# Block-sparse attention with a Fourier mixing layer: k turned by DMA instead of by TensorE

## The chip, the cores and the metric

The kernel runs on one core of one Trainium2 chip. The metric is the device time of one execution in microseconds (us). In this document PE is TensorE (matrix products), PEld its weight loads, DVE is VectorE, ACT is ScalarE, POOL is GpSimd, and SP is SyncE, which here only issues DMA transfers.

## The reference

Two parts follow each other. The first is attention for 4 batches, 8 heads, 768 positions and a head size of 64, in which every query sees its own block of 64 keys and the three blocks whose mean key has the highest product with it:

```
k_rep = k.reshape(B, H, 12, 64, D).mean(axis=3)
gate_scores = einsum('bhsd,bhnd->bhsn', q, k_rep), minus 1e9 where the block lies ahead
selected = top 3 blocks by gate_scores, and the own block
scores = (q @ k.T) / sqrt(D) where selected and causal, else -1e9
x = softmax(scores) @ v, heads side by side: [4, 768, 512]
```

The second works on x batch by batch: the real part of a 2-D Fourier transform over positions and channels is added to x (u = x + real(fft2(x))), u is normalised over its 512 channels, and out = u + relu(un @ w_ch1) @ w_ch2, with w_ch1 of [512, 2048] and w_ch2 of [2048, 512].

## The kernel before

The work of attention is cut into 16 pairs of heads, kk = 0 to 15, four pairs to a batch. A pair goes through these stages, each a function of the kernel:

- load_qk and load_v fetch q, k and v of the pair in f32 with the positions on the 128 partitions (six tiles of 128 positions), over the SP queue. The buffers of q, k and v hold two pairs.
- stage_A(kk, who, g) transposes three tiles at a time on PE with an f32 identity (line 279): who = 0 is q, who = 1 is k. For k, DVE sums each block of 64 columns into kr12 (line 292) and three or four copies by ACT, the fourth by DVE for the pairs before EARLY = 7, cast the transposed k to f16 into kI (lines 309 and 311). kI is the weight operand of the scores: rows 0 to 63 are k, rows 64 to 75 hold for each block n the value -60000 in the columns of block n (IndN, loaded once into each of three slots).
- stage_B makes the gate scores: q's transpose times the block sums. For the pairs before SPLIT = 8 both are f32 (line 323, five matmuls). From pair 8 on q and the sums, scaled by 64, are each split into two f16 parts (lines 287, 288, 304 and 305), and the products are ten f16 matmuls (line 331) and one more addition on DVE. DVE then takes the largest eight of each query and head (line 340) and turns the comparison with the third into a 0/1 mask gmp.
- stage_C transposes the mask on PE (line 354, gt) into the rows 64 to 75 of qg, the moving operand of the scores, so that an unselected block gets -60000 added.
- stage_S computes one of three score sections of a head (line 386) into one of two PSUM buffers (sc), and ACT takes the exponential (line 391). For the pairs before EARLY the causal triangle is added by PE (line 390), later DVE multiplies it in (line 397).
- stage_AV multiplies by v (line 412) with a column of ones for the sum, DVE divides, and fold prepares the Fourier transform's symmetric halves on POOL or DVE.

When a batch has its four pairs, the mixing part follows as a chain of units: stage_S1 (line 480 and 484) and stage_S2 (507, 508, 515) are the transforms, stage_N the norm, stage_T the transposes of the normed rows (562), then bulk units stage_M1 (ha and hb, line 578) and stage_M2 (ch, line 592) for the two products with w_ch1 and w_ch2.

The order of the instructions on PE and POOL is written out by the kernel (a manual schedule). The main loop goes through the pairs; each pair has six slots p = 0 to 5 with one score section, and a table says in which slot the stages of the neighbouring pairs stand:

```
USUAL = dict(A1=0, AV1=1, A0=2, C=3, AV0=4, B=5)
NORM = dict(A1=4, AV1=1, A0=5, C=3, AV0=4, B=6)
```

A1 is stage A for k of pair kk + 2, A0 the same for q with the loads of pair kk + 4 behind it, B the gates of pair kk + 2, C the masks of pair kk + 1. NORM holds in pair NORM_SLOT = 6, where batch 0 is normed. Between them filler(kk, half) pulls units from the chain and from the bulk list. A chain unit is ready when a planner's clock (feed.now) has gone on by a given gap since its predecessor; each slot advances that clock by its listed costs, and by PACE = 1.4 at least. So before the first batch is normed no bulk unit exists, and PE does attention and the chain alone.

DMA transfers are issued in the order of the queues: SP has the loads of q, k and v, the Fourier constants and the outputs; POOL has the masks, the weights w_ch1 (after pairs 2 and 4) and w_ch2 (after pairs 6 and 7). POOL also casts q and v to f16 (lines 240 and 235).

## Time and profile before

| what | value |
|---|---|
| median of three runs | 332.51 us (332.3 to 333.19) |
| the profiled execution's own time | 332.94 us |
| its span, first to last instruction | 331.2 us |
| busy: PE, DVE, ACT, POOL | 311.9, 235.7, 180.3, 84.7 us |
| f32 transposes of k on PE | 96 at 284 ns mean |
| casts of k into kI on ACT and DVE | 57 at 475 ns, 7 at 559 ns |
| reductions of k on DVE | 32 at 551 ns |

A PE instruction of the profile contains its own way through the array, and the next one starts before it ends. So the mean length is not what it costs; the distance between the starts of two neighbours is. A line of a group gives its busy time, the mean length of one and the idle time that its engine had just before it, with what ended that idle time. The stretch up to about 87 us and the rest differ: in the first PE has only attention and the first batch's chain to do.

### The profile page before, as it was taken

How to read it: one execution, taken by the hardware profiler on the slowest of the kernel's cores; microseconds unless marked ns; L12 is line 12 of the kernel's file. 1: busy time of each engine (PE TensorE's matmuls, PEld its weight loads, DVE VectorE, ACT ScalarE, POOL GpSimd, SP SyncE). 2: the span in 40 equal slices, each digit the busy share in tenths (PEclk: the TensorE clock that was granted, in tenths of full speed). 3: DMA queues.
4: the chain of work that ended last, by engine and by line, in shares of the span. 5: the costliest groups of instructions: out<-in, count | busy, mean ns of one | idle time of the engine just before them, and what ended most of it. 6: DMA issues, size and time to landing. Idle time of an engine off the chain costs nothing.

```text
span 331.2 us, 7008 instructions
## 1 busy us (share of the span) xinstructions
PE 311.9 (94%) x2712; PEld 202.9 (61%) x2712; DVE 235.7 (71%) x750; ACT 180.3 (54%) x276; POOL 84.7 (26%) x137
## 2 busy tenths in 40 slices
PE   8799998997889989998999989999999999999995
PEld 3567776876656666555666666656666654556442
DVE  3778889689776898999765898998457588433211
ACT  3188889789965855428486754535764302244000
POOL 8545573352481120504032030502030000000000
PEclk9999999998999999999999999999999999999999
DMA  8997999990799242425324000010000011100021
GB/s 203 230 256 186 246 136 226 155 221 7 165 188 181 54 96 75 103 70 136 99 48 97 2 0 35 32 65 32 34 2 0 2 64 63 65 1 2 32 95 63
DMA packets 85312, 31.18 MB, mean 94 GB/s; under 512 B 77736, under 2 KB 81136, under 8 KB 85280
## 3 DMA queue, kind: packets, MB, share of 16 engines
q1 hardware_dynamic: 79984, 25.88, 31.4%
q0 software_dynamic: 3552, 4.40, 8.5%
q10 hardware_dynamic: 1744, 0.46, 0.6%
q8 instruction: 21, 0.34, 0.4%
q14 instruction: 11, 0.09, 0.1%
HBM read 28.63 MB, written 6.29 MB: 105 GB/s over the span
## 4 chain that ended last, share of the span: by engine, by line
PE 73%; DVE 16%; ACT 7%; issue 1%; POOL 1%; DVEq 0%; ACTq 0%
PE ch L592 22%; PE ha L578 14%; PE sc L386 8%; PE hb L578 7%; PE av L412 5%; ACT kI L311 4%; PE g L323 3%; PE za L480 2%; DVE mx L340 2%; DVE ptl L397 2%; ACT ptl L391 2%; PE tp L279 2%; PE warm L365 2%; PE gt L354 2%; PE mx L507 2%; PE mx L508 2%
## 5 line engine op out<-in xcount | busy, mean ns | idle before, releaser
L391 ACT ACTIVATE ptl<-sc 128x896 f16<-128x896 f32 x96 | 87.3, 919 | 45.9 <-PE sc L386 36.6
L592 PE MATMUL ch<-w_sb,hT 128*128 128x512 f16 x384 | 91.4, 379 | 0.5 <-DVE qT L288 0.5
L578 PEld LDWEIGHTS <-w_sb 128*128 128x128 f16 x512 | 48.8, 97 | 38.6 <-issue 4.7
L578 PE MATMUL ha<-unT,w_sb 128*128 128x512 f16 x256 | 65.7, 378 | 1.8 <-DVE hT L583 1.4
L386 PE MATMUL sc<-qg,kI 76*128 76x512 f16 (+3 forms) x256 | 54.8, 306 | 3.6 <-ACT ptl L391 3.6
L592 PEld LDWEIGHTS <-hT 128*128 128x128 f16 x384 | 36.2, 97 | 35.1 <-issue 0.6
L581 ACT ACTIVATE hT<-ha 128x512 f16<-128x512 f32 x64 | 38.1, 597 | 33.5 <-PE ha L578 33.4
L583 DVE TENSOR_SCALAR hT<-hb 128x256 f16<-128x256 f32 x64 | 26.8, 421 | 28.9 <-PE hb L578 28.7
L578 PE MATMUL hb<-unT,w_sb 128*128 128x256 f16 x256 | 38.4, 272 | 1.1 <-ACT hT L581 0.7
L429 POOL TENSOR_TENSOR fs<-x 128x384 f16<-128x384 f16 x12 | 10.9, 909 | 105.5 <-DVE x L418 91.8
L386 PEld LDWEIGHTS <-kI 76*128 76x128 f16 x256 | 24.0, 100 | 20.3 <-issue 2.8
L311 ACT CAST kI<-tp 64x384 f16<-64x384 f32 x57 | 27.1, 475 | 14.6 <-DVE kr L292 13.6
L595 DVE TENSOR_TENSOR u<-ch,u 128x512 f32<-128x512 f32 x24 | 16.5, 685 | 19.9 <-PE ch L592 19.6
L412 PE MATMUL av<-v,ptl 128*128 128x65 f16 x672 | 26.2, 195 | 0.0
L412 PEld LDWEIGHTS <-ptl 128*128 128x128 f16 x672 | 24.8, 98 | 2.0
L292 DVE TENSOR_REDUCE kr<-tp 128x6 f32<-128x384 f32 x32 | 17.2, 551 | 7.0 <-PE tp L279 7.0
L397 DVE TENSOR_TENSOR ptl<-ptl,ut 128x384 f16<-128x384 f16 x36 | 16.0, 479 | 6.1 <-ACT ptl L391 5.7
L553 ACT ACTIVATE x<-u,nmr,rstd 128x512 f16<-128x512 f32 x12 | 8.9, 806 | 17.7 <-DVE nmr L546 17.6
L418 DVE TENSOR_TENSOR x<-av,rcp 128x384 f16<-128x384 f32 x32 | 17.8, 557 | 0.9
L390 PE MATMUL sc<-ltri,id 128*128 128x128 f16 x84 | 18.4, 219 | 0.0
L240 POOL COPY qg<-qT 64x768 f16<-64x768 f16 x16 | 14.4, 902 | 12.1 <-ACT qT L287 11.6
L520 DVE BATCH_NORM_STATS2 bst<-u 128x6 f32<-128x512 f32 x24 | 16.6, 692 | 1.2 <-ACT u L516 0.7
(112 smaller groups left out, 422.9 us busy)
## 6 DMA issues: line engine op xcount, KB each, us to landing
vn<-in_v_dram SPq DMA_DIRECT2D x32, 192.0 KB, 3.3
out_dram<-u SPq DMA_DIRECT2D x24, 256.0 KB, 2.0
kn<-in_k_dram SPq DMA_DIRECT2D x30, 192.0 KB, 3.3
qn<-in_q_dram SPq DMA_DIRECT2D x30, 192.0 KB, 3.4
w_sb<-in_moe_w_ch_dram POOLq DMA_DIRECT2D x8, 256.0 KB, 7.0
w_sb<-in_moe_w_ch_dram POOLq DMA_DIRECT2D x4, 512.0 KB, 9.5
cs_sb<-c_CS SPq DMA_DIRECT2D x1, 289.5 KB, 4.9
ss_sb<-c_SS SPq DMA_DIRECT2D x1, 289.5 KB, 5.2
```

The source lines that it names most:

```text
L292: nc.vector.tensor_reduce(out=d["kr12"][:, 6 * g:6 * g + 6], in_=ps.rearrange("p a (x c) -> p a x c", x=2), axis=mybir.AxisListType.X, op=ADD)
L311: nc.scalar.copy(out=dst, in_=src_)
L386: nc.tensor.matmul(sp[:, co:co + (a1 - a0)], d["kI"][e][0:76, 128 * jt:128 * (jt + 1)], d["qg"][e][0:76, a0:a1], start=True, stop=not diag)
L390: nc.tensor.matmul(sp[:, co:co + 128], id16, ltri, start=False, stop=True)
L391: nc.scalar.activation(out=pt[:, SEC * s:SEC * (s + 1)], in_=sp[:, 0:SEC], func=AF.Exp, scale=0.125 if kk < SPLIT else 0.125 / QS)
L397: nc.vector.tensor_tensor(out=dg, in0=dg, in1=um, op=MULT)
L412: nc.tensor.matmul(av[:, st, 0:65], pt[:, o:o + 128], d["v16"][:, e, jt, 0:65], start=(cnt == 0), stop=(cnt == 20))
L418: nc.vector.tensor_tensor(out=x_b[:, :, 64 * h:64 * h + 64], in0=av[:, :, 0:64], in1=rcp.to_broadcast([128, NST, 64]), op=MULT)
L578: nc.tensor.matmul(hp_, w1_sb[:, dt, 128 * it:128 * (it + 1)], unT[:, dt, c0:c1], start=(dt == 0), stop=(dt == NDT - 1))
L581: nc.scalar.activation(out=hT[:, c0:c1], in_=hp_, func=AF.Relu)
L583: nc.vector.tensor_scalar(out=hT[:, c0:c1], in0=hp_, scalar1=0.0, scalar2=None, op0=mybir.AluOpType.max)
L592: nc.tensor.matmul(cps, x["hT"][it][:, 128 * st:128 * (st + 1)], w2_sb[:, it, :], start=(it == 0), stop=(it == NIT - 1))
```

## The change

From pair 2 (KDMA) on, stage A is not done for k. Instead turn_k lets POOL cast k to f16 into ks, a buffer of [128 positions, 2 heads, 6 tiles, 128 columns] in one slot, of which the first 64 columns are k and the next 12 hold the block indicators (IndT, loaded once); one transposing DMA on the SP queue writes both into kI, which is now one tile of [128, 2, 768] in each of its three slots. stage_R computes the block sums on PE: for each of the six tiles an f32 matmul with k as the weights and a [128, 2] pattern of ones as the moving operand. Both stand where A1 stood.

SPLIT becomes 2, so the gates of pairs 2 to 7 also use f16 parts, and q of these pairs goes through ACT and DVE as from pair 8 on; the triangle that PE adds for pairs 2 to 6 is scaled by 64 with id64. NORM_SLOT goes from 6 to 7 and PACE from 1.4 to 1.15. v16 has three slots in place of four, the gate scores gsb and mx8 one in place of two, and the warm-up operand lies in w1's buffer. The list TURNED, which would turn the normed rows by DMA, is empty, so stage_T, the chain's gaps and the filler's sums are as before.

```diff
-    kI_t = [[const([128, S], F16, f"kI_{e}_{sl}") for sl in range(3)] for e in range(2)]
-    v16_t = [const([128, 2, NST, 66], F16, f"v16_{sl}") for sl in range(4)]
+    kI_t = [const([128, 2, S], F16, f"kI_{sl}") for sl in range(3)]
+    ks_t = [const([128, 2, NST, 128], F16, f"ks_{sl}") for sl in range(1)]
+    ind2 = const([128, 2], FP, "ind2")
+    id64 = const([128, 128], F16, "id64")
+    v16_t = [const([128, 2, NST, 66], F16, f"v16_{sl}") for sl in range(3)]
...
-    NORM_SLOT = 6
-    SPLIT = 8
+    NORM_SLOT = 7
+    SPLIT = 2
+    KDMA = 2
+    TURNED = ((), (), (), ())
...
+    def turn_k(kk):
+        ks, kn = ks_t[0], P[kk]["kn"]
+        nc.gpsimd.tensor_copy(out=ks[:, :, :, 0:64], in_=kn.rearrange("p s e d -> p e s d"))
+        nc.sync.dma_start_transpose(kI_t[kk % 3].rearrange("p e (s c) -> p (e s) c", c=128),
+                                    ks.rearrange("p e s c -> p (e s c)"))
+        P[kk]["kI"] = [kI_t[kk % 3][:, e, :] for e in range(2)]
+
+    def stage_R(kk):
+        kn = P[kk]["kn"]
+        rps = pst([128, NB], f"r_{kk}")
+        for st in range(NST):
+            nc.tensor.matmul(rps[:, 2 * st:2 * st + 2], kn[:, st, :, :].rearrange("p h d -> p (h d)"),
+                             ind2, start=True, stop=True)
+        block_sums(kk, rps)
...
-        gsb = apool.tile([128, NG, 2, NB], FP, tag="gsb", name=f"gsb_{kk}")
+        gsb = apool.tile([128, NG, 2, NB], FP, tag="gsb", name=f"gsb_{kk}", bufs=1)
...
-                nc.tensor.matmul(sp[:, co:co + 128], id16, ltri, start=False, stop=True)
+                nc.tensor.matmul(sp[:, co:co + 128], id16 if kk < SPLIT else id64, ltri,
+                                 start=False, stop=True)
...
-    PACE = 1.4
+    PACE = 1.15
...
-        for sl in range(3):
+        for sl in range(KDMA):
             for e in range(2):
-                nc.gpsimd.dma_start(kI_t[e][sl][64:64 + NB, :], dr["IndN"].ap())
+                nc.gpsimd.dma_start(kI_t[sl][64:64 + NB, e, :], dr["IndN"].ap())
...
+        for t in ks_t:
+            nc.gpsimd.memset(t[:, :, :, 64 + NB:128], 0.0)
+        for t in ks_t:
+            for e in range(2):
+                nc.sync.dma_start(t[:, e, :, 64:64 + NB], dr["IndT"].ap().rearrange("(st p) n -> p st n", p=128))
+        nc.gpsimd.tensor_scalar(out=id64, in0=id16, scalar1=QS, scalar2=None, op0=MULT)
...
                 if p == at["A1"] and kk + 2 < NK:
-                    main(stage_AA, 0.7, kk + 2, 1)
+                    if kk + 2 < KDMA:
+                        main(stage_AA, 0.7, kk + 2, 1)
+                    else:
+                        turn_k(kk + 2)
+                        main(stage_R, 0.7, kk + 2)
```

block_sums holds what stage A did with the sums before: for pairs 0 and 1 it copies them into kr24, for the others it splits the sums, times 64, into the f16 parts krx; stage_R lets it read the sums from PSUM.

## The prediction

> **What bounds the kernel now.** I read the page's slices first, then the sums by stretch, the groups, the timeline of TensorE (PE) in one early pair, and the chain of waits.
>
> ```profile
> PE   8799998997889989998999989999999999999995
> PEclk9999999998999999999999999999999999999999
> DMA  8997999990799242425324000010000011100021
> ```
> PE is nearly full everywhere, but "busy" counts the drain of each matmul, so gaps are read from start times below. The DMA engines are nearly full for the first quarter only. PE's clock dips once, in the tenth slice.
>
> ```profile
> 20.00:28.00 8.00, 7.62 (x99) 5.91 (x98) 6.14 (x26) 6.68 (x10) 2.48 (x3) 1.00 0.85 191
> 28.00:36.00 8.00, 7.31 (x99) 5.98 (x98) 6.62 (x27) 6.75 (x10) 4.19 (x5) 1.00 0.92 238
> 72.00:86.00 14.00, 11.92 (x131) 9.53 (x130) 11.72 (x50) 12.24 (x21) 1.79 (x2) 0.88 0.28 64
> 86.00:331.00 245.00, 234.93 (x1871) 143.22 (x1871) 169.69 (x501) 117.49 (x183) 42.55 (x56) 1.00 0.25 62
> ```
> Columns: length, then busy us of PE, PEld, DVE, ACT, POOL, granted clock, DMA share, GB/s. There are two stages. Up to the first ha matmul (86.95 us in the timeline) no feed-forward work exists, and the attention pairs follow each other every 8 us, with PE and ACT both short of full. From there filler keeps PE full to the end.
>
> Two groups of the page (engine, operation, names, shape, count, then busy us, mean ns, and idle before with its releaser) belong to k alone, and ACT's copies wait for DVE's reduction:
>
> ```profile
> L311 ACT CAST kI<-tp 64x384 f16<-64x384 f32 x57 | 27.1, 475 | 14.6 <-DVE kr L292 13.6
> L292 DVE TENSOR_REDUCE kr<-tp 128x6 f32<-128x384 f32 x32 | 17.2, 551 | 7.0 <-PE tp L279 7.0
> ```
> From the timeline of PE (start, length) I take what a group costs: the start of the next minus its own, since the lengths overlap. From the chain of waits (start, length) I take what holds an early pair.
>
> ```profile
> 31.80 1.25 PE L323 MATMUL g<-kr,qT 128*128 128x24 f32 x10
> 32.88 0.38 PE L386 MATMUL sc<-qg,kI 76*128 76x512 f16 x1
> ...
> 33.38 0.82 PE L279 MATMUL tp<-id,kn 128*128 128x128 f32 x6
> 34.04 0.38 PE L386 MATMUL sc<-qg,kI 76*128 76x512 f16 x1
> ```
> ```profile
> 34.22 0.47 DVE kr L292
> 34.71 0.47 ACT kI L311
> 35.20 0.48 ACT kI L311
> 35.70 0.47 ACT kI L311
> 36.17 0.82 ACT ptl L391
> ```
> The last fence is the chain of waits: in each early pair it runs through the reduction of k and three kI copies on ACT before the next exponential, 1.9 us of an 8.0 us period (the g groups on that chain start at 23.93, 31.96 and 39.92). PE then waits for the exponential that frees a score buffer.
>
> **The change, part by part.** Pairs 2 to 15 lose stage A for k; 14 pairs, counted from 0.
>
> Step 1, k's transposes on PE go: six take 34.04 - 33.38 = 0.66 us of PE time (0.11 apart). 14 x 0.66 = -9.2 us.
>
> Step 2, stage R comes: six f32 matmuls with k's block as weights and two moving columns. No such row exists. The nearest is the f32 gate: five matmuls are x10 records, each f32 matmul thus two, and take 32.88 - 31.80 = 1.08 us, again 0.11 a record. A transposition moves 128 columns and a gate 24, at the same spacing, so the f32 weight load sets it and two columns should be no cheaper: 12 x 0.11 = 1.32 us. The ends are 0.66 (one record each) and 1.9 (each record held for its PEld row's 0.15 to 0.19 us). I take 1.32; 14 x 1.32 = +18.5 us.
>
> Step 3, gates of pairs 2 to 7 in f16 parts: ten f16 matmuls took 0.26 us (104.71 to 104.97) against 1.08, so 6 x 0.82 = -4.9 us. PE work over all: +4.4 us. This speaks against the change, since PE is the bound of the longer stage.
>
> Step 4, ACT: per early pair three kI copies of 0.48 go and two qh activations of 0.49 (0.45 back to back) come. Six exponentials at 0.92 and 0.9 make 6.4 us, from 6.75. From pair 7 on all four copies go, 1.9 us a pair. DVE loses two reductions (1.1 us) and one kI copy (0.56); the q parts cost what the q copies cost; the f16 gates add one add (0.28) and some 0.5 us of small operations.
>
> Step 5, an early pair anew. PE in order: S, R, S, AV, S, q's transposes, S, gt, S, AV, S, g, with a score section S at 0.5, AV 0.64, transposes 0.66, gt 0.4, R 1.32, g 0.26: 6.9 us. Laid against ACT (qh twice after q's transposes, two score buffers), the last section waits for the fourth exponential by about 0.3 us and the next pair starts 7.3 us after this one. It was 8.0.
>
> Step 6, the first stage. First scores stand at 16.66, 24.85, 32.88, 40.84, 48.73, 62.22, 73.43 and 84.75 us for pairs 0 to 7, the first ha at 86.95. The order of instructions puts the first ha four sections later than before (PACE makes the planner's clock slower, NORM_SLOT moves pair 7's stages): into the fifth section of pair 7. Estimates: pair 0 7.5; pairs 1 to 3 7.3 each; pair 4 with both S1 units (54 matmuls at 0.083) 12.0; pair 5 with three S2 units (0.66 each) 9.3; pair 6 with three more, where ACT has exponentials, qh, three u copies at 0.6 and three norms at 0.8, 10.5; pair 7 up to the first ha, with six T units, R and two AV, 7.3. 16.66 + 7.5 + 21.9 + 12.0 + 9.3 + 10.5 + 7.3 = 85.2 us, -1.8 us. The wait for the norm at 76.6 us (1.56) and the half clock after it (0.50 from 80 to 82 us) should shrink: four sections now lie between the last S2 unit and the first T.
>
> Step 7, the second stage. Four sections, two AV, a gt and a gate have moved out: 4 x 0.39 + 1.28 + 0.28 + 0.27 = -3.4. Pairs 10 to 15 pay R for transposes: 6 x 0.66 = +4.0. PE's waits there sum to 6.4 us, all behind DVE or ACT (hT 3.6 of it, then kI's neighbour unT); with both lighter by 1 to 2 us a pair I take 2.0 off (ends 0 and 5). Together -1.4 us.
>
> Step 8, Pool: a cast of k, nearest row the v cast at 0.83 us, in front of fold, whose own wait for DVE (8.3 us longest) covers it. At the start an ISA instruction that stood ahead of the first fold (line 429) moves ahead of id64's scaling, from 24.5 us to some 8; it was hidden in a 4.1 us gap, so it costs at most that, and the first q cast (8.89) has until the first scores at 16.66. The loads of the 12 indicator columns add two issues on SP, like oth at 0.76 each, in front of pair 2's loads, which were needed at 17.2 and landed 3.3 us after 11.2.
>
> Step 9, the transposing DMA, on SP behind v's load and the Pool cast, with the k and q loads of two pairs later queued behind it. It writes kI two pairs (14.6 us) before the scores read it, and k's later loads have as much. 393 KB: at the best slice's 256 GB/s 1.5 us, at 191 GB/s 2.1, at kn's rate (two halves, 0.5 to issue, 3.3 to landing) 3.8, at the weight loads' (256 KB in 7.0) 10.5. I take 2.1, the row with the same early traffic; no wait on the path then. The Trainium skill (VectorE: DVE Perf Modes, The three transpose paths) gives 1309 ns for one 128x128 f16 block by DMA against 390 ns on TensorE; twelve blocks one after the other would be an estimate of 15.7 us. Its page DMA: Bandwidth & Descriptors (Latency and other measured facts) gives 261 GB/s for DMA transposes, an estimate of 1.5 us. No run here shows either yet.
>
> Slots cut to one or three (gsb, mx8, v16) cost nothing: their users follow on the same engine, or AV of three pairs back is done a section earlier.
>
> Sum: -1.8 - 1.4 = -3.2 us on a span of 331.2. The profiled execution took 332.94 (1.74 around the span), 0.43 above the median 332.51. So 329.7 in its terms, 329.4 as a median.
>
> **Rivals.**
> (a) The DMA engines fill up, the slower side. Shares times lengths over the first 86 us (0 to 20 at 1.03, 0.85, 0.92, 0.92, 18 us at 0.99, 10 at 1.06, 14 at 0.28) make 74.4 us. Eight transposes (pairs 2 to 9) have 10.8 us of room, plus some 8 us of w1's second half that can land after 85 us: 2.35 us each are free, and 2.75 eat the whole gain. For it: landings of up to 9.8 us already occur for kn. Against: the median is 3.3. At 3.8 us it costs 8 x 1.45 = 11.6: 341.
> (b) The same with a transpose at 10.5 us: 8 x 8.15 = +65, 395. The Trainium skill's price for a block (page and section as in step 9) would put it at 8 x 13.35 us, an estimate of 436.
> (c) The early pairs keep their 8 us, because another wait takes kI's place (score buffers, mx on DVE), and the late waits stay: then PE's 4.4 us are paid in full, 336.9. For it: PE work in an early pair falls by only 0.2 us. Against: the chain above passes through the very copies that go.
> (d) Stage R at 0.66: second stage 4.0 less, early pairs about 0.3 shorter (ACT's 6.4 then sets them): 324. Against: the equal spacing in step 2.
>
> **How the numbers follow.** Forecast 0.48 (its own range 326.5 to 332.5), (a) 0.20, (b) 0.04, (c) 0.13, (d) 0.13, 0.02 for nothing of these. A measurement can tell 0.3%, 1.0 us. Below 331.5: 0.41 of the forecast, (d), and 0.04 of (a): 0.58. Within: 0.06 and 0.02 of (a), 0.08. Slower: 0.34. From (d)'s far side to (a) is 322 to 341.
>
> **What would show it.** Early pairs 7.3 us apart; R's 12 records 0.11 apart; first ha near 85 us, no clock below 0.8 around 80 us; transposes landing in 2 to 4 us with none of PE's waits naming a DMA; PE's late waits near 4 us. The forecast is wrong if score matmuls wait for kI's DMA, if DMA share stays near 1 beyond 72 us, or if R takes other than 1.3 us.

## The result, and the profile after

The changed kernel takes 345.48 us (median of four runs, 344.77 to 347.88) where the kernel before takes 332.67 us on the same chip (332.3 to 333.19): a ratio of 1.036, 95% interval 1.029 to 1.043. It is slower by 12.8 us by the medians, by 12.0 by the ratio. The ratios here are the record's own estimate and leave out executions that ran over 1.5% above the fastest of their kernel, so they differ a little from the quotient of the medians. The forecast was 329.4 us with a range to 341; time and sign were both missed. The profiled execution took 345.93 us, with a span of 344.15.

The slices of the changed kernel's page, as before:

```profile
PE   8799997799599799999999989999999999999995
PEclk9958999999679999999999999999999999999999
DMA  9999999999999984445634102011000011100021
```
The transfer engines are full for fourteen slices (120 us), not for the first quarter. TensorE's clock is down in the third and fourth slice and again in the eleventh and twelfth.

The sums by stretch (length, then busy us of PE, PEld, DVE, ACT, POOL, granted clock, DMA share, GB/s):

```profile
20.00:28.00 8.00, 8.00 (x38) 5.82 (x36) 1.70 (x6) 3.60 (x5) 3.09 (x4) 0.52 1.11 206
28.00:36.00 8.00, 8.00 (x117) 6.55 (x114) 5.47 (x26) 6.44 (x9) 2.53 (x4) 1.00 1.21 222
52.00:62.00 10.00, 6.90 (x94) 5.60 (x92) 9.42 (x33) 7.73 (x11) 3.16 (x6) 1.00 1.14 154
86.00:100.00 14.00, 9.28 (x93) 7.44 (x94) 11.64 (x42) 8.56 (x12) 8.21 (x13) 0.73 1.05 178
100.00:344.00 244.00, 235.55 (x1844) 144.56 (x1841) 156.39 (x463) 100.35 (x148) 40.23 (x52) 0.99 0.32 72
```
Three of the early stretches are bad for three different reasons: 20 to 28 us has full work but half a clock, 52 to 62 has gaps, 86 to 100 has both. From 100 us on nothing is lost that was not lost before.

First scores of pairs 0 to 7 stand at 19.02, 30.39, 37.44, 44.49, 51.53, 67.80, 76.78 and 86.16 us, the first ha at 100.24. Up to it the kernel has lost 13.3 us against the kernel before (86.95), and from there to the end it has gained 0.3 (243.9 after 244.2). From the distances between the starts of PE's instructions (taken as work up to 1.05 times what that form usually takes, and as lost beyond it), PE has 304.2 us of work in place of 300.0. From 16 us to the first ha it has 64.5 us of work and 19.7 lost; before, 59.4 and 11.6.

An early pair in PE's timeline (start, length):

```profile
37.14 0.41 PE L361 MATMUL g<-krx,qT 128*128 128x48 f16 x10
37.44 0.38 PE L416 MATMUL sc<-qg,kI 76*128 76x512 f16 x1
...
37.94 1.45 PE L339 MATMUL r<-ind,kn 128*128 128x2 f32 x12
39.25 0.38 PE L416 MATMUL sc<-qg,kI 76*128 76x512 f16 x1
```
Stage R takes 39.25 - 37.94 = 1.31 us, the f16 gates 0.30, and no instruction of this pair waits: the pair takes 7.05 us (37.44 to 44.49) in place of 8.0. What the change was costed for, it does.

The four long waits of PE before the first ha (the bracket is the idle time ahead of the instruction and what ended it):

```profile
16.06 0.46 PE L384 MATMUL gt<-id,gmp 128*44 128x128 f16 x5 [1.52 <-DVE gmp L376]
58.64 0.38 PE L416 MATMUL sc<-qg,kI 76*128 76x512 f16 x1 [1.95 <-ACT ptl L422]
63.29 0.92 PE L511 MATMUL za<-ss_sb,ft 128*128 128x193 f16 x9 [2.18 <-POOL ft L466]
90.61 0.61 PE L597 MATMUL unt<-id,x 128*128 128x128 f16 x4 [3.91 <-DVE x L580]
```
None names a transfer. They stand at the mask of pair 0, twice in pair 4 (a score section, then the first S1 of batch 0), and at the first T of batch 0, behind the norm (pair 7). The exponential that ended the second started at 57.69 us, since ACT did two copies of fold ahead of it. Around the first and the last wait the granted clock is 0.5: from 17.4 to 27.6, 89.1 to 95.9 and 99.3 to 102.7 us, 20.5 us in all, of which 10.2 are lost. Before the change it was 3.4 us in this stage (79.7 to 83.1), and the wait at the first T was 1.56 us:

```profile
78.20 0.40 PE L562 MATMUL unt<-id,x 128*128 128x128 f16 x4 [1.56 <-DVE x L549]
```

Behind the third wait stands a transfer after all. Pool in pair 4, and below it the SP queue at the same time:

```profile
60.93 0.82 POOL L244 CAST v<-vn 128x768 f16<-128x768 f32 x1 [6.47 <-PE sc L420]
62.23 0.82 POOL L330 CAST ks<-kn 128x768 f16<-128x768 f32 x1 [0.48 <-DMA kI<-ks]
63.02 0.21 POOL L466 TENSOR_TENSOR ft<-fs 128x6 f16<-128x6 f16 x1
```
```profile
47.18 1.50 SPq L239 DMA_DIRECT2D vn<-in_v_dram  x2
50.75 5.73 SPq L331 DMA_TRANSPOSE kI<-ks  x1
56.61 4.16 SPq L231 DMA_DIRECT2D kn<-in_k_dram  x2
```
The profile puts Pool's 6.47 us down to PE, whose matmul was done long before; the second half of this v, issued by 48.7 us, lands at 60.72. It is beside the first half of w1, which Pool issued from 47.64 to 49.89. In Pool's order the two small sums for S1 (ft, 0.21 us) come behind the casts of v and k. And a transposing DMA holds SP for 5.73 us here, for 2.3 to 7.5 us in the first nine and for 1.4 us in the last five, from 128 us on, when few transfers are left; its row in the list of transfers is

```profile
kI<-ks SPq DMA_TRANSPOSE x14, 4.5
```
a median of 4.5 us from issue to landing, where the forecast took 2.1 (11.4 us for the one at 50.75, 3.6 for the last five).

The last wait, read in the chain of waits (start, length): DVE between the statistics of batch 0 and the normed rows.

```profile
84.83 0.67 DVE vr L568
...
85.53 0.49 DVE qg L387
...
86.04 0.33 DVE yi L569
...
86.40 0.50 DVE qg L387
...
86.92 0.32 DVE yi L571
...
87.47 0.53 DVE t L574
88.00 0.47 DVE x L449
88.46 0.41 DVE t L575
```
The norm is ten operations on [128, 6] that depend on each other. In DVE's timeline of the kernel before they ran with nothing in between (start, length):

```profile
75.71 0.17 DVE L537 TENSOR_SCALAR vr<-stat 128x6 f32<-128x6 f32 x1
75.91 0.17 DVE L538 TENSOR_SCALAR yi<-vr 128x6 int32<-128x6 int32 x1
76.11 0.17 DVE L540 TENSOR_SCALAR yi<-yi 128x6 int32<-128x6 int32 x1
```
and x could be written 1.9 us after vr. Now two copies of masks, a reciprocal and the product with it, two gate sums and five searches for the largest eight stand between them (eleven operations, 3.07 us), and by the timeline vr itself takes 0.75 us in place of 0.17. From vr to x it is 5.3 us.

### The profile page after: what moved, and what is told of

Read it like the earlier page. It is cut to its first block, busy times and chain, and to the rows that moved or that the text cites. A ratio compares the mean times of both kernels' runs of the same rounds, so it can differ in the third digit from the quotient of the medians.

```text
span 344.1 us, 7185 instructions
## 1 busy us (share of the span) xinstructions
PE 322.7 (94%) x2796; PEld 212.2 (62%) x2796; DVE 228.1 (66%) x741; ACT 161.4 (47%) x235; POOL 94.0 (27%) x149
## 4 chain that ended last, share of the span: by engine, by line
PE 82%; DVE 13%; ACT 2%; issue 2%; POOL 1%; DVEq 0%; POOLq 0%; ACTq 0%
PE ch L626 24%; PE ha L612 14%; PE sc L416 9%; PE hb L612 7%; PE av L443 5%; PE r L339 5%; PE warm L395 3%; PE tp L288 2%; PE za L511 2%; PE unt L597 2%; DVE ft L466 2%; PE ya L515 1%; PE gt L384 1%; PE mx L538 1%; PE mx L539 1%
## 5 line engine op out<-in xcount | busy, mean ns | idle before, releaser
L612 PE MATMUL ha<-unT,w_sb 128*128 128x512 f16 x256 | 66.6, 382 | 2.1 <-DVE hT L617 1.6
L416 PE MATMUL sc<-qg,kI 76*128 76x512 f16 (+3 forms) x256 | 57.4, 317 | 2.5 <-ACT ptl L422 2.2
L416 PEld LDWEIGHTS <-kI 76*128 76x128 f16 x256 | 25.1, 104 | 17.3 <-issue 2.5
L249 POOL COPY qg<-qT 64x768 f16<-64x768 f16 x28 | 24.1, 860 | 21.6 <-ACT qT L296 20.8
L339 PEld LDWEIGHTS r<-ind,kn 128*128 128x128 f32 x168 | 21.4, 202 | 0.5
L339 PE MATMUL r<-ind,kn 128*128 128x2 f32 x168 | 21.1, 254 | 0.0
L244 POOL CAST v<-vn 128x768 f16<-128x768 f32 x16 | 13.2, 823 | 26.1 <-DMA vn<-in_v_dram 19.0
L428 DVE TENSOR_TENSOR ptl<-ptl,ut 128x384 f16<-128x384 f16 x36 | 14.2, 425 | 8.2 <-ACT ptl L422 8.2
```

Of the source, the lines that this page charges most:

```text
L249: nc.gpsimd.tensor_copy(out=d["qg"][e][0:64, :], in_=d["qt" if kk < SPLIT else "qh"][64 * e:64 * e + 64, :])
L339: nc.tensor.matmul(rps[:, 2 * st:2 * st + 2], kn[:, st, :, :].rearrange("p h d -> p (h d)"), ind2, start=True, stop=True)
L416: nc.tensor.matmul(sp[:, co:co + (a1 - a0)], d["kI"][e][0:76, 128 * jt:128 * (jt + 1)], d["qg"][e][0:76, a0:a1], start=True, stop=not diag)
L612: nc.tensor.matmul(hp_, w1_sb[:, dt, 128 * it:128 * (it + 1)], unT[:, dt, c0:c1], start=(dt == 0), stop=(dt == NDT - 1))
```

## The experiments

In the tables of results each ratio is against the kernel before in runs of the same chip, with its 95% interval. In the expectations "a head of k, q or v (96 KB)" should read 192 KB. Executions of the kernel before that enter the ratios spread from 332.3 to 337.25 us in these runs, so differences under 1 us decide nothing.

### First set: transfers, plan or clock

T1: the transposes crowd the transfers, so v lands late and Pool's sums and folds with it. T2: the new plan (NORM_SLOT, PACE) makes the wait at the norm. T3: a pause of PE costs half its clock afterwards.

a_turn_three, the transposing DMA for three pairs only:
```diff
-        nc.sync.dma_start_transpose(kI_t[kk % 3]..., ks...)
+        if kk < 5:
+            nc.sync.dma_start_transpose(kI_t[kk % 3]..., ks...)
```


> Edit: the transposing DMA is issued for pairs 2 to 4 only; the Pool cast of k, stage R and all else stay, so from pair 5 on the scores read whatever k the slot of kI holds (k of an older pair), which changes what is computed and not the work of any engine. Three theories. T1 (transfers): the transposes share the DMA engines with w1 and the loads of v, v lands late, so Pool's casts and folds slip and PE waits for ft before S1 (pair 4: 16.3 us long, 4.3 over the forecast) and for x before the first T (3.9 us, and half clock behind it, 6.8 in all). Then pairs 4 and 7 fall back: first ha near 90 us in place of 100.2, a total of 334 to 337. T2 (planner): NORM_SLOT 7 and PACE 1.15 put the first T too near to the norm: the first ha stays near 100, total 344 to 346. T3 (clock at the start): pair 0 lasts 11.4 us at a clock of 0.5 for lack of PE work before it; also no change from this edit, 344 to 346.

b_old_plan:
```diff
-    NORM_SLOT = 7
+    NORM_SLOT = 6
-    PACE = 1.15
+    PACE = 1.4
```


> Edit: NORM_SLOT 6 and PACE 1.4 as before the change, k still turned by DMA. T1 (transfers): the same transfers meet the same w1, v is late all the same; total 343 to 347. T2 (planner): the wait of 3.9 us for x and the half clock behind it go, and the first ha comes four sections earlier: near 91 us, total 336 to 339. T3 (start): no change, 344 to 346.

c_gates_only, no pair turned:
```diff
-    KDMA = 2
+    KDMA = 16
-        for sl in range(KDMA):
+        for sl in range(min(3, KDMA)):
```


> Edit: no pair is turned by DMA (KDMA 16), so PE transposes k and ACT and DVE copy it as before; the f16 gates from pair 2 on, NORM_SLOT 7 and PACE 1.15 stay, and so do the two loads of the indicator columns. PE work: 14 pairs lose R (1.32) and get six transposes (0.66): 9.2 us less than in the changed kernel, 4.9 less than before. T1 (transfers): without them the first ha is at 87 to 90 us and the total 326 to 330. T2 (planner): the first ha stays near 97 to 100 with a wait for x, total 336 to 340. T3 (start): pair 0 stays at 11 us and first scores at 19: 2 to 4 us on top of either.

d_warm, in the prologue ahead of stage C of pair 0:
```diff
-        stage_W(5)
+        stage_W(13)
```


> Edit: thirteen warm-up products in place of five before stage C of pair 0, so that PE has work through the 1.5 us in which it waits for the mask gmp. T3 (clock at the start): a pause of 1.5 us costs PE half of its clock for the next 6 to 8 us; without the pause pair 0 lasts 8 us in place of 11.4 and the total is 342 to 343. Without T3 (the half clock has another reason): pair 0 stays at 11 us, and the total is 345 to 347, since the eight products can push the mask's transposes back by up to 1.7 us. T1 and T2 say nothing of it.

| run | median us | ratio | pair 4, us | wait for ft | wait for x | first ha |
|---|---|---|---|---|---|---|
| changed kernel | 345.48 | 1.036 (1.029 to 1.043) | 16.3 | 2.2 | 3.9 | 100.2 |
| a_turn_three | 344.31 | 1.029 (1.021 to 1.037) | 20.0 | 1.6 | 3.6 | 98.3 |
| b_old_plan | 352.91 | 1.054 (1.047 to 1.062) | 24.8 | 7.4 | 3.3 | 101.5 |
| c_gates_only | 342.69 | 1.023 (1.017 to 1.029) | 16.9 | none | 3.1 | 96.1 |
| d_warm | 347.83 | 1.036 (1.027 to 1.046) | 23.4 | 3.9 | 3.1 | 101.8 |

T1 in its simple form falls: a took 344.3, and c, without one transposing DMA and with 9 us less for PE to do than in the changed kernel, is still 2.3% slower than the kernel before and has the wait for x in full. Its median of 342.69 is above T2's 336 to 340 too (by the ratio it would be 340.3 beside the 332.67 of the first table), and b contradicts both: on the old plan the turned kernel is worse, and its wait for x stays. In a the longest wait in pair 4 is for a load of k: PE waited 3.49 us for the k of pair 6 at 47.6 us, in front of R, with three transposes done and w1 in the queues.

d agrees with T3 where it was aimed. With PE busy through the pause the clock is 1.00 in this stretch of d_warm, and pair 0 lasts 7.2 us in place of 11.4:

```profile
20.00:28.00 8.00, 8.00 (x99) 6.28 (x99) 5.14 (x21) 6.05 (x8) 4.12 (x5) 1.00 1.13 199
```
But pair 0 also lasted 7.2 to 7.3 us in a, b and c, which have the pause (1.0 to 1.4 us) and kept their clock, so d alone does not show it. The total of 342 to 343 that T3 expected did not come: d lost the gain again in pair 4, behind a wait of 3.08 us for k.

### Second set: one part at a time on the kernel before

before_again is the kernel before, unchanged.

> The kernel before, unchanged, for a trace beside the next three. In the first trace of before a head of k, q or v (96 KB) lands every 0.68 us while the queue is full; in those of the changed kernel and of all four variants, with or without transposes, every 0.80 to 0.90. T4 (this execution): the slower rate belongs to the chip or the moment, and here too a head takes 0.8 to 0.9 us; total 333 to 336. T5 (the kernel): it belongs to the layout of the changed kernel, and here a head takes 0.68 again; total 332 to 334.

e_before_f16 (edits to the kernel before; the planner's price of a gate is held as it was):
```diff
-    SPLIT = 8
+    SPLIT = 2
-    main(stage_B, 1.05 if kk + 2 < SPLIT else 0.35, kk + 2)
+    main(stage_B, 1.05 if kk + 2 < 8 else 0.35, kk + 2)
```


> Edit to the kernel before: SPLIT 2, so the gates of pairs 2 to 7 use f16 parts; k is still transposed by TensorE, and NORM_SLOT 6, PACE 1.4, the planner's price of a gate and all buffers stay. TensorE loses 4.9 us of work. T2 (planner): the plan of before is the better one, early pairs take 7.4 us as they did without transposes, so 327 to 330. T6 (the f16 gates themselves): the q parts put 1 us per pair more on ACT, DVE and Pool in the stretch up to the norm, k's copies are late and the pauses of TensorE are those of the variant with gates only; 338 to 343.

f_before_plan (edit to the kernel before):
```diff
-    NORM_SLOT = 6
+    NORM_SLOT = 7
-    PACE = 1.4
+    PACE = 1.15
```


> Edit to the kernel before: NORM_SLOT 7 and PACE 1.15 alone. T2 (planner): the copies of the masks and the gates then stand between the operations of the norm on DVE, TensorE waits 3 us or more for x before the first T and loses half its clock for 3.5 or 7 us behind it: first ha at 93 to 97 us, total 337 to 342. T6 and T4: the plan as such costs nothing, 331 to 335.

g_fill_norm (edit to the changed kernel, in stage_T, ahead of the first transposes of batch 0):
```diff
+            if b == 0:
+                stage_W(16)
```


> Edit to the changed kernel: sixteen warm-up products (3.4 us) on TensorE right before the first T of batch 0, in the pause in which it waits 3.9 us for x. They take nothing from the pause itself. T3 (clock): behind a pause of 1.5 us or more TensorE runs at half clock for 3.5 or 7 us (89 to 96 us and 99 to 103 in the changed kernel), so with the pause filled 3.5 to 5 us are gained: 340 to 342. If the half clock has another reason (the load of the first units, for one): 344 to 348.

| run | median us | ratio | wait for x | vr to x on DVE, other operations in it | first ha |
|---|---|---|---|---|---|
| before_again | 332.73 | 1.0005 (0.998 to 1.003) | 1.6 | 1.9 us, none | 89.3 |
| e_before_f16 | 334.40 | 1.003 (1.000 to 1.006) | 2.3 | 2.0 us, one | 89.1 |
| f_before_plan | 341.07 | 1.025 (1.021 to 1.028) | 3.2 | 4.4 us, ten | 96.4 |
| g_fill_norm | 347.50 | 1.040 (1.033 to 1.047) | 0.3 | (filled) | 100.2 |

f gives the largest single price: the two numbers of the plan alone, on a kernel that is otherwise the one before, cost 2.5%, 8.2 us. T2 is right for that kernel, and the mechanism is the one expected. By the starts of PE's instructions 17.3 us are lost from 16 us to the first ha and 11.4 behind it, where before_again loses 12.2 and 9.4; so a smaller part of the price lies behind the first ha. DVE in f_before_plan, and PE's wait behind it:

```profile
81.65 0.17 DVE L537 TENSOR_SCALAR vr<-stat 128x6 f32<-128x6 f32 x1
81.73 0.55 DVE L288 SCALAR_TENSOR_TENSOR qT<-tp,qT 128x384 f16<-128x384 f32 x1
82.20 0.46 DVE L538 TENSOR_SCALAR yi<-vr 128x6 int32<-128x6 int32 x1
82.58 0.55 DVE L288 SCALAR_TENSOR_TENSOR qT<-tp,qT 128x384 f16<-128x384 f32 x1
83.04 0.50 DVE L540 TENSOR_SCALAR yi<-yi 128x6 int32<-128x6 int32 x1
83.57 0.48 DVE L357 COPY qg<-gt 12x640 f16<-12x640 f16 x1
```
```profile
86.69 0.61 PE L562 MATMUL unt<-id,x 128*128 128x128 f16 x4 [3.16 <-DVE x L549]
```
After every step of the norm DVE takes an operation of the pair's own attention, half a microsecond each; the clock then is halved from 85.75 to 92.6 us.

e shows that the f16 gates gain nothing: 4.9 us less work for PE and +0.3%. The early pairs do get shorter (7.2 to 7.5 us apart), and the waits of pair 4 (1.55 us for a copy of k on ACT) and of the norm take it back. T2's gain of several us did not come, nor did T6's loss of several us.

g says what the clock is worth. The pause was filled and the granted clock is 1.00 where the changed kernel had 0.73:

```profile
86.00:100.00 14.00, 13.14 (x164) 9.14 (x163) 13.39 (x45) 11.21 (x17) 8.95 (x13) 1.00 1.30 195
```
From the first T to the first ha it took 7.1 us in place of 9.6. The total of 340 to 342 that was expected did not come: pair 4 took 19.7 us in this execution, with half a clock from 58.75 to 69. A saving of 2.5 us in one place can be lost to one pause elsewhere.

before_again settled T4 against T5: in it a head of 192 KB lands every 0.68 us while the queue is full, by the landing times of the trace, as in the first profile of before; in e and f too. In all kernels with the changed kernel's buffers, c among them, it took some 0.8 to 0.9. So the layout did it. The new ind2 has 8 bytes per partition, for which the allocator takes 32, and everything behind it, with the buffers of q, k and v, starts 32 bytes past a multiple of 64.

### Third set: the buffers, and the plan once more

h_aligned (edit to the changed kernel):
```diff
-    ind2 = const([128, 2], FP, "ind2")
+    ind2 = const([128, 16], FP, "ind2")[:, 0:2]
```


> Edit to the changed kernel: the pattern of ones, ind2, gets 64 bytes per partition in place of 8 (of which the allocator makes 32), so every buffer behind it, among them those of q, k and v, starts at a multiple of 64 bytes as it did before the change, in place of 32 more than one. T5a (place of the buffers): a 256-byte piece written from a multiple of 64 bytes goes faster, a head of q, k or v lands every 0.67 us in a full queue in place of 0.80 to 0.90. By 60 heads in the first 86 us that is 10 to 13 us of queue time; the waits for ft and for landed k or v in pair 4 go and the first scores come 1 us earlier; the wait for x before the first T, which comes with the plan, stays: 338 to 341. T5b (another part of the layout): heads stay at 0.8 to 0.9, 344 to 348.

i_before_shifted (edit to the kernel before):
```diff
+    pad = const([128, 8], FP, "pad")
+    nc.vector.memset(pad, 0.0)
     kr24_t = [...]
```


> Edit to the kernel before: an unused pad of 32 bytes per partition ahead of kr24, which moves the buffers of q, k and v to 32 bytes past a multiple of 64, and nothing else. T5a (place of the buffers): heads land every 0.85 to 0.90 us; 10 to 12 us more of queue time against 10.8 us of room that the shares of the DMA engines left in the first 86 us, so 333 to 337, with first scores 0.5 to 1.5 us later. T5b: heads stay at 0.67, 332 to 334.

j_aligned_old_plan: the edits of h_aligned and b_old_plan.

> Edit to the changed kernel: ind2 with 64 bytes as in the aligned variant, and NORM_SLOT 6 and PACE 1.4 as before the change. With the buffers 32 bytes off the old plan was the worst of all (352.9), with waits of 1.0 for kI, 1.7 for kn and 7.4 for ft. T5a and T2 together: those waits go with the alignment, the wait for x goes with the plan, and what is left is TensorE's 4.4 us of added work against early pairs of 7.1 us: 329 to 335. If the transposes still crowd the transfers: 340 to 350, with a wait for ft of over 2 us.

k_aligned_slot6: the edit of h_aligned and NORM_SLOT = 6.

> Edit to the changed kernel: ind2 with 64 bytes, NORM_SLOT 6, PACE left at 1.15. It splits the plan's two numbers. If the table of the norm (NORM_SLOT) makes the wait for x, by letting the masks, AV's divisions and the gates of pair 6 onto DVE between the operations of the norm: the wait falls to 1.6 us or less, 333 to 337. If PACE makes it: as the aligned variant with NORM_SLOT 7, 338 to 341.

| run | median us | ratio | a head lands every | pair 4, us | wait for ft | wait for x |
|---|---|---|---|---|---|---|
| h_aligned | 343.89 | 1.030 (1.024 to 1.035) | 0.67 us | 16.3 | 2.3 | 3.9 |
| i_before_shifted | 334.35 | 1.002 (1.000 to 1.005) | 0.88 us | 15.2 | none | 1.6 |
| j_aligned_old_plan | 349.49 | 1.049 (1.042 to 1.056) | 0.67 us | 20.5 | 4.7 | 2.9 |
| k_aligned_slot6 | 344.99 | 1.037 (1.032 to 1.041) | 0.67 us | 22.2 | 3.0 | 3.5 |

T5a is shown from both sides: 32 bytes of padding and nothing else make a head take 0.88 us in place of 0.67, and 56 more bytes in ind2 undo it. The median way from issue to landing of v shows it too, in the kernel before and then in i_before_shifted:

```profile
vn<-in_v_dram SPq DMA_DIRECT2D x32, 192.0 KB, 3.3
```
```profile
vn<-in_v_dram SPq DMA_DIRECT2D x32, 192.0 KB, 4.2
```
Of the time it is a small part, 0.8 us in i and some 1.5 in h: neither interval excludes much less, and the waits of h are those of the changed kernel. The expectation that alignment would clear pair 4 was wrong. j took 349.5 with a wait for ft of 4.7 us, which is its second branch (the transposes still crowd the transfers) and not the 329 to 335 that was thought likely if the waits went. k missed both its branches; its time cannot be told from h's, so at PACE 1.15 the norm's slot alone decides nothing.

### Fourth set: the jam, and the pause

l_w1_later (edit to h_aligned):
```diff
-            if kk in (2, 4):
+            if kk in (4, 5):
                 pool_after(P[kk + 2]["qt"])
-                load_w1(kk // 2 - 1)
+                load_w1(kk - 4)
```


> Edit to the changed kernel: ind2 with 64 bytes as in the aligned variant, and the two halves of w1 loaded after pairs 4 and 5 in place of 2 and 4. In the aligned variant the load of v for pair 5 and 6 was issued at 47.3 us, beside the first half of w1 (47.5 to 49.7) and behind a transpose that held SP 3.2 us; v landed only when Pool had waited 6.6 us, its small sums for S1 came behind that, TensorE waited 1.9 and 2.3 us, and pair 4 took 16.3 us. J1 (a jam of w1, the loads and the transposes): without w1 there pair 4 takes 12 to 13.5 us, the waits for ft fall below 1 us, total 338 to 341, the wait for x before the first T as before. J2 (SP's queue alone, held by the transposes): pair 4 stays at 15 us or more, 342 to 345.

m_before_gap (edit to the kernel before):
```diff
-        t_gap = {0: 4.0, B - 1: 6.0}.get(b, 7.5)
+        t_gap = {0: 5.5, B - 1: 6.0}.get(b, 7.5)
```


> Edit to the kernel before: the planner's gap between the last S2 unit and the first T of batch 0 goes from 4.0 to 5.5, so one more score section and the masks stand in front of the first T. TensorE waited 1.56 us for x there, and its clock halved near by for 3.5 us (79.75 to 83.25). If the pause is the cause and attention fills it: 1.5 to 3 us less, 329.5 to 331.5. If the clock halves for another reason, or the section moved is missed later: 332 to 334.

n_w1_gap: l_w1_later with 7.5 as that gap.

> Edit to the changed kernel: as the variant with w1 later, and the same gap from 4.0 to 7.5 (three slots of 1.15). The wait for x of 3.9 us and two stretches at half clock behind it (10.5 us, of which 5.3 are lost) stand in the aligned variant. J3 (pauses and clock are what is left): both go, 331 to 336. J4 (the turned k costs more than its pauses: TensorE's added 4.4 us of work and the filled transfer queues): 337 to 341.

o_f16_gap: e_before_f16 with 5.5 as that gap.

> Edit to the kernel before: SPLIT 2 as in the variant with f16 gates on the old plan (334.4, with a wait for x of 2.3 us and half clock from 78.75 to 85.75), and the gap 5.5. If the 4.9 us of TensorE's work that the f16 gates save were hidden by that pause and its clock: 328 to 331. If the f16 gates save nothing where they stand, because the pairs up to the norm are bound by ACT and the waits: 331 to 334.

| run | median us | ratio | pair 4, us | first ha | wait for x |
|---|---|---|---|---|---|
| l_w1_later | 342.22 | 1.025 (1.021 to 1.030) | 13.4 | 91.4 | 3.1 |
| m_before_gap | 337.55 | 1.012 (1.010 to 1.015) | 13.5 | 89.7 | 1.6 |
| n_w1_gap | 341.76 | 1.026 (1.023 to 1.030) | 13.4 | 97.2 | 0.6 |
| o_f16_gap | 338.53 | 1.016 (1.011 to 1.020) | 15.3 | 89.0 | 2.1 |

l shows J1 for pair 4: with w1 out of its way it takes 13.4 us in place of 16.3, and no wait for ft is left. PE in this stretch of h_aligned, then of l_w1_later:

```profile
52.00:62.00 10.00, 6.80 (x93) 5.51 (x91) 9.27 (x33) 7.64 (x11) 3.01 (x6) 1.00 1.15 152
```
```profile
52.00:62.00 10.00, 9.93 (x143) 9.05 (x141) 8.54 (x30) 6.74 (x12) 6.57 (x12) 1.00 1.02 192
```
The medians differ by 1.7 us, less than the 3 us of the pair: a new wait of 2.47 us for a masked score section (ptl) appeared at 90 us, and the 342.2 us lie just above the 338 to 341 that J1 expected.

Moving the first T back does not work. In m the section that went in front of it brought its two copies of masks onto DVE between the steps of the norm, from vr to x took 2.9 us in place of 1.9, and the wait for x was 1.6 us as before; the later stage lost 13.0 us in place of 9.4; the 337.55 us missed both ranges that were expected. o, with the f16 gates and the same gap, does as m: two copies of masks, 3.0 us from vr to x in place of 2.0, and a total above both its ranges. In n the wait for x went down to 0.6, and PE waited 1.86 us for the mask and 1.88 for a mask's copy in its place; the clock was halved from 83 to 100 us. J3 fell.

### Fifth set: the transposes alone, and the clock alone

p_turn_unused (edit to the kernel before; ks and the target are parts of w2's buffer, which is loaded later, and nobody reads the result; Pool also clears a part of ks once at the start):
```diff
+                    if kk < 6:
+                        nc.gpsimd.tensor_copy(out=ks[:, :, :, 0:64], in_=P[kk + 2]["kn"]...)
+                        nc.sync.dma_start_transpose(w2f[:, 1536:3072]..., w2f[:, 0:1536])
                     main(stage_AA, 0.7, kk + 2, 1)
```


> Edit to the kernel before: for pairs 2 to 7 Pool also casts k and a transposing DMA turns it, in the place in which the changed kernel does, but from and to the part of w2's buffer that is not loaded yet; nobody reads the result, and TensorE, ACT and DVE do all that they did before. So the six transposes and casts are priced by themselves. J1 (they crowd SP, the DMA engines and Pool, v lands late beside w1's first half, and the small sums for S1 behind it): pair 4 takes 2 us or more longer than 13.5 to 15.1, total 335.5 to 340. J5 (a transposing DMA is hidden, as forecast, and the rest of the change makes the loss): 332.5 to 334.5.

q_f16_fill (e_before_f16 and, ahead of the first T of batch 0):
```diff
+            if b == 0:
+                stage_W(9)
```


> Edit to the kernel before: SPLIT 2 (f16 gates for pairs 2 to 7, plan as before) and nine warm-up products (1.9 us) on TensorE right before the first T of batch 0, in the pause of 2.3 us in which it waits for x; the variant without them took 334.4 and ran at half clock from 78.75 to 85.75. T3 (clock): the pause stays, the half clock behind it goes, 3.5 us less: 330.5 to 332. If the half clock has another reason: 333.5 to 335.5. Below 332 it beats both kernels.

| run | median us | ratio |
|---|---|---|
| p_turn_unused | 340.09 | 1.017 (1.012 to 1.021) |
| q_f16_fill | 333.74 | 1.000 (0.998 to 1.002) |

Six transposes and casts, whose result is thrown away, cost the kernel before 1.7%, 5.6 us by the ratio. J5, which was the forecast's step 9, is wrong. Only its times are read here.

q shows the clock with nothing moved but the filling. The stretch behind the norm in e_before_f16, then in q_f16_fill:

```profile
80.00:86.00 6.00, 6.00 (x56) 5.07 (x56) 4.50 (x14) 4.78 (x9) 1.78 (x2) 0.53 0.18 42
```
```profile
80.00:86.00 6.00, 5.01 (x59) 3.48 (x55) 4.42 (x14) 5.32 (x11) 1.78 (x2) 1.00 0.34 77
```
The half clock is gone. The median fell by 0.7 us against 3.5 expected, and the kernel ends level with the kernel before. No variant of these runs beats that one.

## Why the prediction was wrong, step by step

Steps 1 to 3, PE's work: right. The transposes of k and q fell from 21.2 to 11.9 us, R takes 18.1 (1.29 a pair, forecast 1.32), the gates fell from 10.6 to 5.7: +3.9 us, with all else +4.2, forecast +4.4.

Step 4, relief of ACT and DVE: right in size (ACT busy 161.4 us after 180.3, DVE 228.1 after 235.7; a busy time counts overlapping lengths once, and the lengths of DVE's instructions added up fell by 12.7, where the step's terms make some 13.5).

Step 5, an early pair: 7.05 us after 8.0, forecast 7.3.

Step 6, the first stage: here it failed. The first ha was forecast at 85.2 and stands at 100.24, 15.0 us later. Term by term: the start was forecast unchanged at 16.66 and came 2.4 later; pair 0 took 11.4 and not 7.5 (+3.9); pairs 1 to 3 0.8 less; pair 4 16.3 and not 12.0 (+4.3); pairs 5 and 6 1.4 less; pair 7 up to the first ha 14.1 and not 7.3 (+6.8).

- Pair 7. The sentence that failed is that the wait for the norm "should shrink: four sections now lie between the last S2 unit and the first T". It counted what the moved stages put on PE, and not what the same stages put on DVE, where the norm runs: copies of masks, divisions, gate sums. f shows this on the kernel before: ten such operations between the norm's steps, 4.4 us in place of 1.9, a wait of 3.2 us and half a clock behind it. On that kernel the plan is the largest single price, 8.2 us. But putting the old plan back into the changed kernel does not clear the wait: in b and j seven other operations stand between the steps, four of them the split of R's block sums, vr to x takes 3.8 us, and PE waits 3.3 and 2.9 us. DVE in j_aligned_old_plan:

```profile
83.78 0.16 DVE L325 TENSOR_SCALAR krx<-r 64x12 f16<-64x12 f32 x1
83.87 0.15 DVE L571 TENSOR_SCALAR yi<-yi 128x6 int32<-128x6 int32 x1
83.98 0.16 DVE L326 SCALAR_TENSOR_TENSOR krx<-r,krx 64x12 f16<-64x12 f32 x1
```
- Pair 4, and with it steps 8 and 9. "No wait on the path" was wrong for a transposing DMA, and so was the claim that fold's wait for DVE covers Pool's cast of k. kI itself was in time (in b PE waited 0.98 us for it). What came late was another load: v, landing 12 us after its issue, held up beside w1's first half and the transposes; Pool takes its work in order, so S1's small sums waited behind the cast of that v. The price of 2.1 us for a transpose was too low by half (4.5), and its hold on SP, 2.3 to 7.5 us in the first nine, was not costed at all. The Trainium skill's two figures, from which the text had estimates of 15.7 us by the block price (stated for bf16) and 1.5 by the rate, are both away from these 4.5 us, and from the 3.6 of the last five. p prices six of them at 5.6 us, and l takes pair 4 back to 13.4 us by moving w1 alone.
- Pair 0. The half clock was not foreseen, though the trace of before showed a pause of 1.56 us at the norm and half a clock behind it. Whether a pause of 1.4 to 1.5 us at the start halves the clock differs from profile to profile: it did in the changed kernel, g and h (1.52, 1.52, 1.46 us) and not in c, j, k and m (1.43, 1.53, 1.44, 1.52). What made the changed kernel's pause as long as 1.52 is read below.
- The start. Over eleven profiles with the changed kernel's prologue the first scores stand at 18.2 us in the mean (17.2 to 19.4), over eight with that of before at 17.3 (16.7 to 18.1). So some 0.8 of the 2.4 us belong to the kernel and the rest to the two executions compared.

Step 7, the second stage: -0.3 in place of -1.4. Its PE work came out near the forecast (230.8 us after 230.5, forecast +0.6), but the 2.0 us of waits that were to go shrank by 0.5 only.

The rivals. (a), that the transfer engines fill up, had the right place, and one of the prediction's signs of being wrong came true for it: that the DMA share stays near 1 beyond 72 us; it was 1.12 from 72 to 86 us and 1.05 from 86 to 100. Its price for a transpose, 3.8 us for a total of 341, was nearly right; with the 4.5 us measured its sum would give 346.6. That this is near the 345.48 is luck, since the sum holds nothing of the plan, and c loses 7.6 us without one transposing DMA. PE's waits do not name a transfer; the delay reaches PE through Pool's order. (b) and (d) did not occur. Of (c) the early pairs did not keep their 8 us, but the late waits stayed. No rival had the plan as its mechanism, though the diff changes it, and its 8.2 us on the kernel before are more than the forecast's own range allowed for. The slots that were cut are not tested apart; c has them and loses less (7.6 us) than plan and gates together (9.1), so no cost of theirs shows.

The parts do not add up. By the ratios plan 8.2, six transposes and casts 5.6, shift 0.8 and gates 0.9 make 15.5 against 12.0, and stage R in place of PE's transposes of k is in none of them. In one order they can be followed: the plan alone costs 8.2 us (f), with gates, shift and cut slots it is 7.6 (c), and turning k on top brings 12.0, 4.4 more. In the other order it is not so: on the old plan turned k costs 15 us (j after e), and the new plan then takes 5.6 off (h after j), with a wait for ft of 2.3 us in place of 4.7. Which of the two plans is better thus depends on whether k is turned, and no fixed share of the loss belongs to either. Why the old plan suits the turned k so badly stays open. That the turned k would be worth its price on a plan made for it, with w1 elsewhere and the norm alone on DVE, stays open too: l with 1.025 is the nearest that was run.

## What to carry to other kernels

When stages are moved past a short chain of dependent operations, list what they issue on the engine that runs the chain, not only on the one that waits for it. For every transfer added to a queue, ask which load stands behind it, and follow that load through the in-order engine that consumes it, to the last small operation in that line. A pause of TensorE is to be priced with the half clock that can follow it, and a new small constant with the alignment of every buffer behind it.

## What the hardware showed that was not expected

**The clock is set in steps of 3.41 us, and short pauses are enough.** In the clock records of all twenty profiles, between 8 and 112 us, every stretch at half clock is a whole multiple of 3.41 us long (3.41, 6.83 and 10.24 in the changed kernel, 17.07 in n), and the starts of one run's stretches lie whole multiples of 3.41 us apart (17.40, 89.08 and 99.32 in the changed kernel, 21 and 24 steps). So each run has a grid of such steps. Of the steps at full clock in which PE stood idle for over 2.05 us, all 21 were followed by a step at half clock; of those with 1.35 to 2.05 us idle, 16 of 29; of those with less, 6 of 465, and all six came right behind a step that ended a stretch at half clock. This tells part of the chance: the pause of 1.55 us in before_again (78.96 to 80.52) is cut in two by a step's end at 79.7 and left the clock full, while two pauses of 0.77 and 0.46 us within one step halved it at 55.8. The Trainium skill (TensorE: Matmul & The Clock Gate, "Part 1: The HAM clock gate") describes a window of about 3.4 us that runs freely and a clock that is either full or half. The lengths and the grid agree with that. It also says that the clock falls after at least one idle window of some 3.4 us; here 1.4 to 2 us of idle time within one step were enough.

**32 bytes of alignment cost a quarter of the loads' rate.** Pieces of 256 bytes written 32 past a multiple of 64 bytes: 0.88 us for 192 KB, in place of 0.67. The times of the kernels hardly show it.

**Small DVE operations end when Pool's operation ends.** In the changed kernel vr (84.75 for 0.75 us) ends at 85.50, Pool's cast of k at 85.48; two later steps of the norm end at 87.99 and 88.87, Pool's two copies of q at about 88.0 and 88.86. In l_w1_later, where Pool is done at 78.08, the step behind it (t) takes 0.12 us in place of 0.61, and the same operations from vr to x take 4.06 us in place of 5.25. gmp of the early pairs took 0.80 to 0.88 us beside an operation of Pool (14.41, 39.64 and 53.73) and 0.28 without one (19.16, 33.30 and 46.69). The one at 14.41, beside Pool's cast of v (14.33 to 15.15), made the first pause 1.52 us; in h, j, k and m that cast stretches another small operation (kr, to 0.7 to 0.8 us in place of 0.17) and the pause is 1.44 to 1.53, and in before_again and l it falls beside the searches for the largest eight, which keep their length, and the pause is 0.90. The Trainium skill (SBUF — State Buffer, "Who interferes with whom") has a pair of ports that DVE and Pool share and that one of them holds for a whole instruction; DVE needs it in a two-port mode or, beside a Pool operation that reads SBUF, with two inputs in SBUF. The ends and the lengths agree; no edit here took Pool's operation away, so the ports as the reason are read, not shown.
